# Token sums behind the attention output, a second reciprocal in PSUM, two side units moved and the last projection ahead of its fill

## The chip, the cores and the metric

One core of one Trainium2 chip runs the whole program. The metric is the device time in microseconds, the median of three runs. A profile was taken of one more execution; its own time stands beside its span in the table below.

## What is computed

Two branches read the same input `x` (2048 tokens of 512 channels) and are mixed by a gate per token. Branch A is an attention with a recurrent memory: the tokens are cut into 64 segments of 32, each segment is preceded by 8 memory rows, and the first 8 rows of a segment's output are the next segment's memory. Branch B is a layer norm and a two-layer MLP.

```python
g = sigmoid((x * gate_w).sum(-1, keepdims=True))
for s in range(64):                      # 32 heads of 128, one after the other in s
    h = concat([mem, x[32*s:32*s+32]])   # 40 rows
    q, k, v = h @ Wq, h @ Wk, h @ Wv
    p = softmax(mask(q @ k.T * scale))   # memory rows see all, token rows are causal
    o = (p @ v) @ Wo
    mem = o[:8];  outs.append(o[8:])
a = concat(outs)
b = gelu(layernorm(x) @ w1 + b1) @ w2 + b2
out = g * a + (1 - g) * b
```

## The kernel before

**Stages.** First the MLP runs in eight blocks of two token tiles (a tile is 128 tokens, T = 0 to 15) while the attention's weights load. For nine of the tiles (`DEF`) only the hidden layer is computed there and stored in DRAM (`h_dr`); their second layer is later fed into the attention loop as filler work. Then a loop runs over the 64 segments, called steps here (s = 4T + si). All instructions of an engine run in the order in which the program lists them; the order is written by hand, and the framework adds semaphores where two instructions touch the same tile. SyncE (SP) issues nearly all DMAs of the loop, in order too.

**One step.** TensorE (PE) makes q and k for 32 rows (24 tokens and the 8 memory rows; the tile's other 8 tokens per segment, the "left" ones, were made a tile ahead) into the four PSUM banks `U[0..3]`; ScalarE (ACT) casts them, VectorE (DVE) transposes them to `QT` and `KT`. Scores go in two halves of 16 heads to the banks `SbF` and `U[0]`; ACT takes the exponential into `E`; V is made in `X1` and `X2` and cast by ACT into `V`, four casts in all (L834). `E` has 56 columns per head group: columns 40 to 55 belong to the memory rows' queries. Only these are normalised before the output is made:

- `msum(i2)` sums them over the keys by a matmul with ones (`BO`), half 0 into `U[1]`, half 1 into `U[3]`; `mnorm(i2)` on DVE takes the reciprocal (L824) into `RP[i2]` and multiplies `E`'s memory columns by it (L825). `RP[0]` is a piece of the PSUM bank `SbF`, `RP[1]` the SBUF tile `RS`.
- `av` makes p @ v for all 40 rows (L291, L296), half 0 of the heads, then half 1, into the four `U` banks. It uses the normalised memory columns and the token columns as they are.
- `xsums(E, h)` sums the token columns of half h (L715) into a piece of `SbF` called `xs`. `recip_x` then takes their reciprocals into `R` (L727), writes these to DRAM (`r_dr`, L730), loads them back spread over all partitions (`Rb`, L733), and in between loads as many tiles `hm` of the deferred MLP as were used up since (L661). It copies `RP` to `R` (L735), writes the mask into `SbF` again (L260), and adds `R` into `racc` on GpSimd (POOL).
- ACT casts the memory columns of `U` to `UT` (L865) and the raw token columns to `XR` (L721). One step later POOL multiplies `XR` by `Rb` into `UT`'s token columns and into `UL` for the left tokens (`x_norm`, L745).
- `wo_pass` projects `UT` with `Wo` (L160): the memory columns of this step and the token columns of the step before. ACT casts the result to `w` in three pieces, and `new_mem` (L761, then L763 on DVE) turns each into the next step's memory rows `hT`.

**Filler.** Where a chain through ACT and DVE would leave PE idle, the step calls `run(n)`, which advances a generator `fill` made by `side(T, si)`: q, k and v of the left tokens, or the projection of `UL` (`wo_left`), four matmuls of 512 columns a unit. In step 2, where there is no earlier tile, `mlp_units(8)` stands for it: a unit is twice `next(mlp)`, a half of four matmuls of 256 columns into the bank `W` (L689). Beside that a step has two or three single halves. `hm_load4` at step 2's beginning brings four more tiles in one DMA. `WS` places two units behind V, two behind the output and two (one at si = 0) behind the projection; one follows each of the first two `new_mem`.

**The end.** Step 63 stops behind its V. Outside the loop the sums of all 32 rows are made in `SbF`, `UL` gets zeros in its unused columns (L896, POOL), `out_sel` writes the tile before, `wo_left(T, X2)` becomes the filler, DVE takes the reciprocals of all columns (L901) and normalises `E`, and `wo_pass(UT[s % 2])` projects step 62's tokens.

Of the kernel before, what the change touches and what calls it, by code (L numbers as in the profile page):

```python
# [9 lines left out]
FP32 = mybir.dt.float32  # L10
# [18 lines left out]
def kernel(ctx, tc, A_x, A_mem0, A_Wq, A_Wk, A_Wv, A_Wo, A_seg_len, B_x, B_w1, B_b1, B_w2, B_b2, gate_w, out):  # L29
    nc = tc.nc  # L30
    P = 128
    _, S, Dm = A_x.shape
# [8 lines left out]
    SPT = P // seg  # L41
# [32 lines left out]
    ep = early.enter_context(tc.tile_pool(name="ep", bufs=1))  # L74
# [31 lines left out]
    def left_x(T):  # L106
        GL = ew.tile([P, KC, LEFT, SPT], BF16, tag="GL", name="GL")
        nc.gpsimd.tensor_copy(out=GL[:].rearrange("p k c i -> p k i c"), in_=xTs[T][:].rearrange("p k (i t) -> p k i t", i=SPT)[:, :, :, RIDE:seg])
        GLs[T] = GL
# [3 lines left out]
    X1 = lps.tile([P, 512], FP32)  # L113
    X2 = lps.tile([P, 512], FP32)
    SbF = lps.tile([P, 512], FP32)
# [40 lines left out]
    def wo_group(bk, U_, n):  # L156
        j, ih = HORD[n]
        for c in range(4):
            i = 4 * ih + c
            nc.tensor.matmul(bk[32 * c:32 * c + 32, :], lhsT=U_[:, j, i, :], rhs=Wo_sb[:, 4 * i + j, :],  # L160
                             start=(n == 0), stop=(n == NW - 1), tile_position=(0, 32 * c))
# [13 lines left out]
    def left_qk(T, t, hf, bk):  # L175
        for kc in range(KC):
            qk_unit(bk, gl(T), t, hf, kc)
            if kc < KC - 1:
                yield
        def ca():  # L180
            Tb = qk_cast(bk[:])
            dve_q.append(lambda: qk_tr(Tb, QL[T % 2], hf) if t == 0 else kl_tr(Tb, T, hf))
        act_q.append(ca)
        yield
# [6 lines left out]
    def left_v(T, vb, bk):  # L191
        if vb == 0:
            VLs[T] = ew.tile([P, 4, 2, Dh], BF16, tag="VL", bufs=1, name="VL")
        for kc in range(KC):
            v_unit(bk, gl(T), vb, kc)
            if kc < KC - 1:
                yield

        def ca():
            VL = VLs[T]  # L200
            nc.scalar.copy(out=VL[:, :, vb, :], in_=bk[:].rearrange("p (a e) -> p a e", a=4))

            if vb == 1:
                vp_load(T, 0)
        act_q.append(ca)
        yield
# [8 lines left out]
    def wo_left(T, bk):  # L215
        for n in range(NW):
            wo_group(bk, UL[T % 2], n)
            if n < NW - 1:
                yield

        def ca():
            wl = cw.tile([P, Dm], BF16, tag="wl", name="wl")
            nc.scalar.copy(out=wl[:], in_=bk[:])
            wls[T] = wl
        act_q.append(ca)
        yield
# [24 lines left out]
                              in_=QL[T % 2][:].bitcast(FP32).rearrange("p a (l s) b -> p a l s b", s=SPT)[:, :, :, si])  # L251


    RS = ep.tile([P, 32], FP32)
    RP = [SbF[:, 336:368], RS[:]]


    def mask_put(i2):
        c = 4 * EW + (2 * XQ + 2 * M if i2 == 0 else 0)
        nc.vector.tensor_copy(out=(SbF, U[0])[i2][:, 0:c], in_=MkF[:, 0:c])  # L260
# [23 lines left out]
    def av(s, V, E):  # L284
        T, si = divmod(s, SPT)
        Uv = [U[j][:, 0:NG * 40].rearrange("p (i q) -> p i q", q=40) for j in range(4)]
        for i2 in range(2):
            for i in range(4 * i2, 4 * i2 + 4):
                for j in range(4):
                    q = slice(32 * j, 32 * j + 32)  # L290
                    nc.tensor.matmul(Uv[j][:, i, :], lhsT=V[q, i, :], rhs=E[q, i, 8:48],  # L291
                                     start=(i == 0), stop=False, skip_group_check=True, tile_position=(32 * j, 0))
            for j in range(4):
                q = slice(32 * j, 32 * j + 32)
                lo = slice(4 * i2, 4 * i2 + 4)
                nc.tensor.matmul(Uv[j][:, lo, :].rearrange("p i (a b) -> p i a b", b=8)[:, :, 0:5:4, :], lhsT=VP[T % 2][q, si, i2, :],  # L296
                                 rhs=E[q, lo, :].rearrange("p i (a b) -> p i a b", b=8)[:, :, 0:7:6, :],
                                 start=False, stop=True, skip_group_check=True, tile_position=(32 * j, 0))
# [329 lines left out]
    def run(n):  # L628
        for _ in range(n):
            next(fill, None)  # L630

    def chain(*gens):
        for x in gens:
            yield from x

    def side(T, si):
        gens = []
        if si == 2:
            gens = [wo_left(T - 1, X1) if T >= 1 else mlp_units(8)]
        elif T + 1 == NT:  # L640
            gens = [mlp_units(4)] if si < 2 else []
        else:
            gens = [[left_qk(T + 1, 0, 0, X1), left_qk(T + 1, 1, 0, U[3])], [left_qk(T + 1, 0, 1, X1), left_qk(T + 1, 1, 1, U[3])], [],
                    [left_v(T + 1, 0, X1), left_v(T + 1, 1, U[3])]][si]
        return chain(*gens)
# [25 lines left out]
    def mlp_out(T):  # L671
        ct = cw.tile([P, Dm], BF16, tag="o", bufs=1, name="ct")
        nc.vector.tensor_scalar(out=ct[:], in0=W[:], scalar1=omg[:, T:T + 1], scalar2=None, op0=ALU.mult)
        nc.sync.dma_start(c_dr[T * P:(T + 1) * P, :], ct[:])
# [3 lines left out]
    def mlp_outs():  # L678
        while outs:
            mlp_out(outs.pop())  # L680

    def mlp_halves():
        while hms:
            T, fc, hm, n = hms.pop(0)
            mlp_outs()
            for h in range(2):
                cc = slice(256 * h, 256 * h + 256)
                for c in range(4):
                    nc.tensor.matmul(W[32 * c:32 * c + 32, cc], lhsT=hm[:, 32 * c:32 * c + 32], rhs=w2_sb[:, fc, cc],  # L689
                                     start=(fc == 0 and h == 0), stop=(fc == FC - 1), skip_group_check=True, tile_position=(0, 32 * c))  # L690
                if h == 1:
                    owed[0] += n
                    if fc == FC - 1:
                        outs.append(T)
                yield

    def mlp_units(n):
        for _ in range(n):
            next(mlp, None)
            next(mlp, None)  # L700
            yield
# [3 lines left out]
    mlp = mlp_halves()  # L705
# [6 lines left out]
    def xsums(E, h):  # L712

        for c in range(4):
            nc.tensor.matmul(xs[32 * c:32 * c + 32, h, 0:40], lhsT=BO[:, 0:P:4], rhs=E[:, 4 * h + c, 0:40],  # L715
                             start=False, stop=True, skip_group_check=True, tile_position=(0, 32 * c))
# [7 lines left out]
    def recip_x(s):  # L724
# [9 lines left out]
        for i2 in (1, 0):  # L734
            nc.vector.tensor_copy(out=R[:, 32 * i2:32 * i2 + 32], in_=RP[i2])  # L735
        mask_put(0)
# [10 lines left out]
    def wo_pass(U_, cuts=(0, Dm), bk=W):  # L747
        for n in range(NW):
            wo_group(bk, U_, n)
        w = cw.tile([P, Dm], BF16, tag="w", bufs=8, name="w")  # L750
        for a, b in zip(cuts, cuts[1:]):
            nc.scalar.copy(out=w[:, a:b], in_=bk[:, a:b])  # L752
        return w
# [14 lines left out]
    for s in range(nseg):  # L768
        T, si = divmod(s, SPT)
        last = s == nseg - 1  # L770
        hc, hn = hT[s % 3], hT[(s + 1) % 3]
        W1, W2, W3 = WS[si]
        fill = side(T, si)
        if s + 1 < nseg:
            prep_h(s + 1)
# [25 lines left out]
        V = cx.tile([P, NG, Dh], BF16, tag="V", name="V")  # L801
        E = cx.tile([P, NG, EW], BF16, tag="E", name="E")
# [16 lines left out]
        def mnorm(i2):  # L819
            r, e = RP[i2], E[:, 4 * i2:4 * i2 + 4, 40:56].rearrange("p i (a q) -> p i a q", q=8)  # L820
            if i2 == 0:
                m = U[1][:, 320:384].rearrange("p (i a q) -> p i q a", i=4, a=2)
                nc.vector.tensor_reduce(out=r.rearrange("p (i q) -> p i q", q=8), in_=m, axis=AX.X, op=ALU.add)
            nc.vector.reciprocal(out=r, in_=U[3][:, 320:352] if i2 else r)  # L824
            nc.vector.tensor_tensor(out=e, in0=e, in1=r.rearrange("p (i q) -> p i q", q=8).unsqueeze(2).to_broadcast([P, 4, 2, 8]), op=ALU.mult)  # L825
# [32 lines left out]
        run(W1)  # L858
        if s:
            next(mlp, None)  # L860
        xsums(E, 1)
        recip_x(s)
        av(s, V, E)
        for j in (0, 2, 1, 3):
            nc.scalar.copy(out=UT[s % 2][:, j, :, 0:M], in_=U[j][:, 0:NG * 40].rearrange("p (i q) -> p i q", q=40)[:, :, 32:40])  # L865
        x_raw(s)
# [15 lines left out]
        mlp_outs()  # L882
        for _ in fill:
            pass
        if si == 3 and T + 2 < NT:
            left_x(T + 2)
        flush(dve_q, 9)
# [9 lines left out]
    for _ in out_sel(T - 1, X1):  # L897
        pass
    fill = wo_left(T, X2)
    run(3)  # L900
    nc.vector.reciprocal(out=R[:, nx], in_=SbF[:, 0:32 * NG])  # L901
    nc.scalar.activation(out=rmin[:, nx], in_=R[:, nx], func=ACTF.Copy, accum_out=tot[:, 3:4])
    ws[s - 1] = wo_pass(UT[s % 2])
    Rr = R[:, nx].rearrange("p (i q) -> p i q", q=32)
    nc.vector.tensor_tensor(out=E[:, :, 8:40], in0=E[:, :, 8:40], in1=Rr, op=ALU.mult)
    nc.vector.tensor_tensor(out=E[:, :, 0:8], in0=E[:, :, 0:8], in1=Rr[:, :, 0:8], op=ALU.mult)
# [176 lines left out]
```

## Time and profile before

| what | value |
|---|---|
| timed runs, us | 747.28, 747.86, 749.27; median 747.86 |
| profiled execution, us | 750.09 |
| its span, first to last instruction, us | 748.2 |
| granted TensorE clock, mean | 0.997 |
| busy share of the span | PE 98%, ACT 72%, DVE 60%, POOL 33% |
| hardware DMA queue of SP | 60,802 packets, 72.51 MB |

PE's share is the one that counts: an engine that is busy for 98% leaves some 15 us of idle time in all. The busy time of a matmul contains its way through the array, so short holds between small matmuls do not show as idle; they are read from the start times in the timeline.

### The profile page before, as it was taken

The page shows a single profiled execution, that of the slowest core. Times are in us where ns is not written, and L with a number is a line of the kernel's source. Part 1 is how long each engine was busy: PE and PEld are TensorE (multiplying, and loading weights), DVE is VectorE, ACT ScalarE, POOL GpSimd, SP SyncE. Part 2 cuts the span into 40 slices and gives each one's busy share as a digit, 9 for nine tenths or more (in the row PEclk, how much of TensorE's full clock was granted, in tenths as well). Part 3 has the DMA queues.
Part 4 walks back from the last instruction along what each step waited for, and adds up shares of the span by engine and source line. Part 5 has one row for each costly group of instructions (what it writes and reads, how often), then busy time and mean ns, then how long its engine had stood idle before and what let it go on. Part 6 is the DMA issues. An engine that isn't in the chain of part 4 may idle for free. (4 is left out here: it accounts for less than half of the span.)

```text
span 748.2 us, 44010 instructions
## 1 busy us (share of the span) xinstructions
PE 732.8 (98%) x19147; PEld 428.8 (57%) x19147; DVE 448.9 (60%) x1541; ACT 536.7 (72%) x1629; POOL 246.6 (33%) x515
## 2 busy tenths in 40 slices
PE   8999998999999999999999999999999999999997
PEld 5776554556565555555555555555555555555553
DVE  6877554656565555656565665556665656555554
ACT  6777765777777777777777777777777777777664
POOL 4001332332334333343234334243333343333331
PEclk9999999999999999999999999999999999999999
DMA  8999222222222323122321323231322313222221
GB/s 308 343 360 360 84 83 55 69 87 80 78 68 62 97 74 93 47 83 80 93 79 38 96 75 97 69 81 57 92 78 82 85 44 94 69 90 70 85 63 61
DMA packets 61944, 76.82 MB, mean 103 GB/s; under 512 B 26729, under 2 KB 51922, under 8 KB 60210
## 3 DMA queue, kind: packets, MB, share of 16 engines
q1 hardware_dynamic: 60802, 72.51, 31.1%
q8 instruction: 151, 2.47, 1.3%
q0 software_dynamic: 400, 0.92, 0.3%
q10 hardware_dynamic: 544, 0.52, 0.2%
q14 instruction: 47, 0.39, 0.2%
HBM read 60.21 MB, written 7.70 MB: 91 GB/s over the span
## 5 line engine op out<-in xcount | busy, mean ns | idle before, releaser
L134 ACT CAST Tb<-U 128x512 bf16<-128x512 f32 x288 | 168.8, 586 | 82.5 <-PE U L129 76.8
L745 POOL TENSOR_TENSOR UT<-XR,Rb 128x384 bf16<-128x384 bf16 x126 | 114.1, 927 | 324.6 <-DMA Rb<-r_dr 228.0
L129 PEld LDWEIGHTS <-hT 128*32 128x32 bf16 x4096 | 108.8, 97 | 97.8 <-issue 2.0
L129 PE MATMUL U<-Wq_sb,hT 128*32 128x512 bf16 x2048 | 145.9, 382 | 0.4 <-DVE hT L763 0.4
L129 PE MATMUL U<-Wk_sb,hT 128*32 128x512 bf16 x2048 | 145.2, 381 | 0.0
L148 PE MATMUL X<-Wv_sb,hT 128*32 128x512 bf16 x2048 | 142.9, 378 | 0.0
L160 PE MATMUL X<-Wo_sb,UT 128*32 128x512 bf16 x2016 | 120.8, 380 | 0.0
L834 ACT CAST V<-X 128x256 bf16<-128x256 f32 x256 | 88.7, 372 | 16.0 <-PE X L148 1.1
L138 DVE STREAM_TRANSPOSE QT<-Tb 128x256 f32<-128x256 f32 x128 | 57.0, 445 | 71.1 <-ACT Tb L134 70.9
L763 DVE CAST hT<-U 128x8 bf16<-128x8 f32 x126 | 20.8, 167 | 130.9 <-PE U L761 96.6
L160 PEld LDWEIGHTS <-UT 128*32 128x32 bf16 x2048 | 56.4, 96 | 55.7 <-issue 16.6
L721 ACT CAST XR<-U 128x256 bf16<-128x256 f32 x252 | 78.6, 438 | 0.0
L752 ACT CAST w<-X 128x128 bf16<-128x128 f32 x189 | 44.8, 310 | 41.7 <-PE X L160 41.0
L138 DVE STREAM_TRANSPOSE KT<-Tb 128x256 f32<-128x256 f32 x128 | 57.0, 445 | 25.9 <-ACT Tb L134 25.9
L737 POOL TENSOR_TENSOR racc<-racc,R 128x128 f32<-128x128 f32 x63 | 28.8, 457 | 105.7 <-DVE R L735 101.1
L148 PEld LDWEIGHTS <-hT 128*32 128x32 bf16 x2048 | 45.2, 95 | 20.6
L689 PE MATMUL W<-w_sb,hm 128*32 128x256 bf16 x728 | 50.5, 273 | 3.6 <-DMA hm<-h_dr 3.6
L865 ACT CAST UT<-U 128x64 bf16<-128x64 f32 x252 | 35.4, 227 | 25.9 <-PE U L296 25.9
L745 POOL TENSOR_TENSOR UL<-XR,Rb 128x128 bf16<-128x128 bf16 x126 | 51.5, 430 | 0.0
L809 ACT ACTIVATE E<-U 128x64 bf16<-128x64 f32 (+1 forms) x128 | 35.0, 273 | 9.3 <-PE U L271 0.4
L484 PEld LDWEIGHTS <-w_sb 128*128 128x128 bf16 (+1 forms) x352 | 34.1, 100 | 10.4
L160 PE MATMUL X<-Wo_sb,UL 128*32 128x512 bf16 x512 | 38.7, 379 | 1.0 <-POOL UL L896 1.0
(184 smaller groups left out, 1250.5 us busy)
## 6 DMA issues: line engine op xcount, KB each, us to landing
Rb<-r_dr SPq DMA_DIRECT2D x63, 512.0 KB, 3.9
Wv_sb<-in_A_Wv_dram SPq DMA_DIRECT2D x4, 1024.0 KB, 7.5
Wq_sb<-in_A_Wq_dram SPq DMA_DIRECT2D x4, 1024.0 KB, 8.5
Wk_sb<-in_A_Wk_dram SPq DMA_DIRECT2D x4, 1024.0 KB, 8.4
Wo_sb<-in_A_Wo_dram SPq DMA_DIRECT2D x4, 1024.0 KB, 12.6
VP<-VL SPq DMA_DIRECT2D x64, 64.0 KB, 3.7
hm<-h_dr SPq DMA_DIRECT2D x91, 32.0 KB, 2.6
c<-c_dr SPq DMA_DIRECT2D x16, 128.0 KB, 4.6
```

The lines of the kernel that those rows point to most:

```text
L129: nc.tensor.matmul(bk[32 * j:32 * j + 32, :], lhsT=G[:, kc, :], rhs=W5[t][:, kc, h0:h1, j, :], start=(kc == 0), stop=(kc == KC - 1), tile_ ...
L134: nc.scalar.copy(out=Tb[:], in_=bk.rearrange("p (a b e) -> p a e b", a=8, b=2))
L138: nc.vector.transpose(out=dst[:, 8 * hf:8 * hf + 8, c0:c0 + 32, :].rearrange("p a r b -> p a (r b)").bitcast(FP32), in_=Tb[:].rearrange("p ...
L148: nc.tensor.matmul(bk[32 * j:32 * j + 32, :], lhsT=G[:, kc, :], rhs=Wv5[:, kc, 4 * vb:4 * vb + 4, j, :], start=(kc == 0), stop=(kc == KC - ...
L160: nc.tensor.matmul(bk[32 * c:32 * c + 32, :], lhsT=U_[:, j, i, :], rhs=Wo_sb[:, 4 * i + j, :], start=(n == 0), stop=(n == NW - 1), tile_po ...
L689: nc.tensor.matmul(W[32 * c:32 * c + 32, cc], lhsT=hm[:, 32 * c:32 * c + 32], rhs=w2_sb[:, fc, cc], start=(fc == 0 and h == 0), stop=(fc = ...
L721: nc.scalar.copy(out=XR[:, j], in_=U[j][:, 0:NG * 40].rearrange("p (i q) -> p i q", q=40)[:, :, 0:32])
L745: nc.gpsimd.tensor_tensor(out=out[:, :, 4 * h:4 * h + 4, o:o + b - a], in0=XR[:, :, 4 * h:4 * h + 4, a:b], in1=Rb[:, h, :, :, r:r + b - a] ...
L752: nc.scalar.copy(out=w[:, a:b], in_=bk[:, a:b])
L809: nc.scalar.activation(out=E[:, 4 * i2:4 * i2 + 4, c], in_=Sb[i2][:, :, c], func=ACTF.Exp, scale=scale)
L834: nc.scalar.copy(out=V[:, i0:i0 + 2, :].rearrange("p i e -> p (i e)"), in_=(X1, X2)[vb][:, 256 * h:256 * h + 256])
L865: nc.scalar.copy(out=UT[s % 2][:, j, :, 0:M], in_=U[j][:, 0:NG * 40].rearrange("p (i q) -> p i q", q=40)[:, :, 32:40])
```

## The change

Four edits:

1. Second half's token sums: `xsums(E, 1)` and `recip_x(s)` come behind `av(s, V, E)` instead of ahead of it, in every step but the last.
2. `RS` is dropped; both memory reciprocals are pieces of `SbF` (columns 336 to 367 and 368 to 399).
3. Step 2's filler has six units instead of eight. Of the four halves that leave it, one comes at the end of step 3 and three at the end of step 4, behind the filler's rest, each followed by `mlp_outs()`, which scales and stores a finished tile of the MLP.
4. At the end `run(3)`, twelve matmuls of the `UL` projection, comes behind `wo_pass` instead of ahead of DVE's reciprocal.

```diff
-    RS = ep.tile([P, 32], FP32)
-    RP = [SbF[:, 336:368], RS[:]]
+    RP = [SbF[:, 336 + 32 * i:368 + 32 * i] for i in range(2)]
...
-            gens = [wo_left(T - 1, X1) if T >= 1 else mlp_units(8)]
+            gens = [wo_left(T - 1, X1) if T >= 1 else mlp_units(6)]
...
+        av(s, V, E)
         xsums(E, 1)
         recip_x(s)
-        av(s, V, E)
         for j in (0, 2, 1, 3):
             nc.scalar.copy(out=UT[s % 2][:, j, :, 0:M], in_=U[j][:, 0:NG * 40].rearrange("p (i q) -> p i q", q=40)[:, :, 32:40])
...
         for _ in fill:
             pass
+        for _ in range({SPT - 1: 1, SPT: 3}.get(s, 0)):
+            next(mlp, None)
+            mlp_outs()
         if si == 3 and T + 2 < NT:
...
     fill = wo_left(T, X2)
-    run(3)
     nc.vector.reciprocal(out=R[:, nx], in_=SbF[:, 0:32 * NG])
     nc.scalar.activation(out=rmin[:, nx], in_=R[:, nx], func=ACTF.Copy, accum_out=tot[:, 3:4])
     ws[s - 1] = wo_pass(UT[s % 2])
+    run(3)
```

The order of the instructions, first on DVE from the first sum of the memory columns to the mask, in a step of the loop's middle, before (the names in brackets are the engines whose semaphores a row waits for; `DVE_49` is its own; `U_119` is `U[1]`, `U_121` is `U[3]`):

```order
L823 TENSOR_REDUCE SbF<-U_119 128x32 [waits DVE_49,PE_49,Activation_49]
L824 RECIPROCAL SbF<-SbF 128x32 [waits DVE_49]
L825 TENSOR_TENSOR E<-E,SbF 128x4x16 [waits DVE_49]
L824 RECIPROCAL RS<-U_121 128x32 [waits PE_49]
L825 TENSOR_TENSOR E<-E,RS 128x4x16 [waits DVE_49,Activation_49]
L726 TENSOR_REDUCE SbF<-SbF 128x2x8 [waits PE_49]
```

The same rows now (lines are one less):

```order
L822 TENSOR_REDUCE SbF<-U_119 128x32 [waits DVE_49,PE_49,Activation_49]
L823 RECIPROCAL SbF<-SbF 128x32 [waits DVE_49]
L824 TENSOR_TENSOR E<-E,SbF 128x4x16 [waits DVE_49]
L823 RECIPROCAL SbF<-U_121 128x32 [waits DVE_49,PE_49]
L824 TENSOR_TENSOR E<-E,SbF 128x4x16 [waits DVE_49,Activation_49]
L725 TENSOR_REDUCE SbF<-SbF 128x2x8 [waits DVE_49,PE_49]
```

The rows stand in the same order; the second reciprocal and the token sums' reduction each wait for DVE's own semaphore as well, the reciprocal for the product ahead of it.

On SP, the DMAs from step 2's `recip_x` to step 3's, before:

```order
L730 DMA r_dr_78<-R 16x64
L661 DMA hm<-h_dr_69 128x128 x2
L661 DMA hm<-h_dr_70 128x128
L733 DMA Rb<-r_dr_78 128x1024
L674 DMA c_dr<-ct 128x512
L730 DMA r_dr_79<-R 16x64
L661 DMA hm<-h_dr_70 128x128 x4
L733 DMA Rb<-r_dr_79 128x1024
```

And now:

```order
L729 DMA r_dr_78<-R 16x64
L660 DMA hm<-h_dr_69 128x128 x2
L660 DMA hm<-h_dr_70 128x128
L732 DMA Rb<-r_dr_78 128x1024
L729 DMA r_dr_79<-R 16x64
L660 DMA hm<-h_dr_70 128x128 x2
L732 DMA Rb<-r_dr_79 128x1024
L673 DMA c_dr<-ct 128x512
```

Step 3 loads two tiles instead of four, and the store of the first finished deferred tile (`c_dr`) moves from behind step 2's loads to behind step 3's.

## Prediction

> **What bounds the kernel now.** I read the page first, then the windows of single steps, then the PE's waits, then the timeline of one quiet step, one disturbed step, the start and the end.
>
> ```profile
> span 748.2 us, 44010 instructions
> PE 732.8 (98%) x19147; PEld 428.8 (57%) x19147; DVE 448.9 (60%) x1541; ACT 536.7 (72%) x1629; POOL 246.6 (33%) x515
> ```
>
> TensorE is busy for 98% of the span and executes in order, so the time changes only by what PE waits for, or by the speed at which it is clocked. The profiled execution took 750.09 us, 1.85 us more than its span; the median of the timed runs is 747.86 us, 2.23 us less. I make the sum against the profile and put it on the median; the rivals come back to those 2.23 us. About 0.3% (2.2 us) is what a measurement of this kernel can tell from no change.
>
> ```profile
> core 0: us, PE busy (x) PEld busy (x) DVE busy (x) ACT busy (x) POOL busy (x), PEclk, DMA share, GB/s
> 97.08:109.35 12.27, 10.61 (x325) 6.51 (x320) 6.56 (x21) 6.69 (x22) 4.24 (x8) 1.00 0.30 87
> 109.35:123.78 14.43, 12.02 (x292) 6.14 (x288) 5.49 (x20) 7.77 (x24) 5.84 (x12) 0.88 0.25 68
> 300.62:310.81 10.19, 10.19 (x292) 5.78 (x288) 6.29 (x22) 7.67 (x24) 2.95 (x8) 1.00 0.18 66
> ```
>
> These windows run from one step's first score matmul to the next's: step 2, step 3, and step 22 as a quiet one. Steps 2 and 3 are 2.1 and 4.2 us longer than a quiet step. Why, a row of the PE's waits says (total, times, longest):
>
> ```profile
> PE W L689 <- DMA hm<-h_dr: 3.6, 3, 2.4
> ```
>
> **The start: side units.** Timeline of steps 2 to 4 (start, duration, engine, what; in brackets the idle time before it):
>
> ```profile
> 104.89 0.40 PE L689 MATMUL W<-w_sb,hm 128*32 128x256 bf16 x8 [0.89 <-DMA hm<-h_dr]
> 114.32 2.75 SPq L661 DMA_DIRECT2D hm<-h_dr  x4
> 114.94 0.62 PE L148 MATMUL U<-Wv_sb,GL 128*32 128x512 bf16 x8
> 117.96 0.29 PE L689 MATMUL W<-w_sb,hm 128*32 128x256 bf16 x4 [2.41 <-DMA hm<-h_dr]
> 119.13 1.51 PE L129 MATMUL U<-Wq_sb,hT 128*32 128x512 bf16 x12
> 131.12 0.82 PE L129 MATMUL U<-Wq_sb,hT 128*32 128x512 bf16 x12
> ```
>
> A unit is two halves of four matmuls on one `hm` tile. With eight units step 2 uses up all tiles it has. Its last units wait for loads of the same step (104.89), and step 3's third half waits 2.41 us for a tile asked for at 114.32. Soon after, the same twelve matmuls take 1.51 us at 119.13 and 0.82 us a step later: the clock, whose mean in that window is 0.88. That is 14.43 x 0.12 = 1.7 us.
>
> With six units, step 2's last two units go, and with them four halves. The tiles loaded in step 2, which its own last units used, are then left for step 3's halves, so all three waits go: -3.6, and -1.7 for the clock. The four halves come back at the ends of steps 3 and 4, where nothing waits and PE is full: a half is 0.11 us (eight matmuls take 0.40 at 104.89, four 0.29 at 117.96), +0.4. In step 2 their place between the three `new_mem` pieces becomes idle, since these wait for ScalarE's three casts anyway; that step gains only its waits. SP issues two loads fewer in step 3 in front of Rb, and the c_dr store follows Rb; both have a step of slack. Sum of the start: **-4.9 us**, with -5.4 if step 2 shortens by part of the removed halves, and -2.4 if the wait is 1.6 us and the clock stays up, as below.
>
> **The quiet step: reciprocals and sums.** From step 22, in the order DVE, ACT, PE:
>
> ```profile
> 302.45 0.37 DVE L824 RECIPROCAL SbF<-SbF 128x32 f32<-128x32 f32 x1
> 302.86 0.22 DVE L825 TENSOR_TENSOR E<-E,SbF 128x64 bf16<-128x64 bf16 x1
> 302.99 0.35 DVE L824 RECIPROCAL RS<-U 128x32 f32<-128x32 f32 x1
> 303.45 0.23 DVE L825 TENSOR_TENSOR E<-E,RS 128x64 bf16<-128x64 bf16 x1
> ```
>
> ```profile
> 303.15 0.65 ACT L834 CAST V<-X 128x256 bf16<-128x256 f32 x2
> 304.14 0.56 ACT L865 CAST UT<-U 128x64 bf16<-128x64 f32 x4 [0.35 <-PE U L296]
> ```
>
> ```profile
> 303.46 0.20 PE L715 MATMUL SbF<-E,BO 128*32 128x40 bf16 x4
> 303.73 0.34 PE L291 MATMUL U<-E,V 32*128 32x40 bf16 x16
> 304.04 0.62 PE L129 MATMUL X<-Wq_sb,GL 128*32 128x512 bf16 x8
> 304.50 0.40 PE L160 MATMUL X<-Wo_sb,UT 128*32 128x512 bf16 x4
> ```
>
> The second reciprocal starts at 302.99, 0.09 us before the first product ends (302.86 + 0.22 = 303.08): two Vector instructions without a wait between them overlap. Writing into SbF, it must now wait for that product, because the product reads SbF; the rows of the order show this wait in front of it in every step. What such a wait costs, the next pair tells: the product at 303.45 waits for the reciprocal ending 303.34 by a separate semaphore instruction and starts 0.11 us behind it. Where the wait is the instruction's own (302.82 to 302.86) it costs 0.04; the new one has two waits, so I take 0.11.
>
> So: reciprocal at 303.08 + 0.11 = 303.19; 0.37 as the PSUM-to-PSUM row above, to 303.56; product at 303.67, 0.22 as the other product, to 303.89, against 303.68 now. PE's second half of the output starts 0.05 behind the product (303.73), so at 303.94. Now it is also held inside by V's cast, which ends at 303.80; later that is no limit. What the rest then takes, a step shows in which this product came late:
>
> ```profile
> 364.36 0.81 POOL L745 TENSOR_TENSOR UL<-XR,Rb 128x128 bf16<-128x128 bf16 x2
> 364.74 0.51 DVE L825 TENSOR_TENSOR E<-E,RS 128x64 bf16<-128x64 bf16 x1
> 365.31 0.28 PE L291 MATMUL U<-E,V 32*128 32x40 bf16 x16
> 365.55 0.61 PE L148 MATMUL X<-Wv_sb,GL 128*32 128x512 bf16 x8
> 365.66 0.56 ACT L865 CAST UT<-U 128x64 bf16<-128x64 f32 x4 [0.57 <-PE U L296]
> 366.02 1.91 PE L160 MATMUL X<-Wo_sb,UT 128*32 128x512 bf16 x32
> ```
>
> From 365.31 to the next matmul 0.24; so 303.94 + 0.24 = 304.18 against 304.04: **0.14 us later in each step**, and the cast and the projection, 0.36 behind the cast in both steps, move by as much. Nothing later in the step takes it back: all else follows the projection. 63 x 0.14 = +8.8 us.
>
> The sums behind the output: four matmuls, 0.03 us of PE by their issue, inside a stretch that PE spends waiting for UT (304.18 + 0.03 + 0.43 of fill = 304.64, needed at 304.65). I cost them at nothing; uncovered they are 0.03 to 0.13 a step (303.46 to 303.59, where the output begins, is the upper end), 2 to 8 us. Before the output they covered PE time in which it waits for V anyway, so their leaving gains nothing. recip_x, the Rb load and x_norm behind them come 304.18 - 303.46 - 0.14 = 0.58 us later relative to the next step. In the late step above the UT part of x_norm is done at 364.36, 1.66 us ahead of the projection; only the few latest steps can be reached: +0.2, bounds 0 and 1.
>
> The other side of the PSUM reciprocal is that late product itself. Its durations (minimum, median, maximum, ns), and its mean:
>
> ```profile
> L825 DVE TENSOR_TENSOR E<-E,SbF x63: 220/221/223, 78.6 to 725.4; 128x64 bf16<-128x64 bf16 x63
> L825 DVEq EVENT_SEMAPHORE  x63: 21/21/21, 79.1 to 725.9; - x63
> L825 DVE TENSOR_TENSOR E<-E,RS x63: 225/226/873, 79.2 to 726.0; 128x64 bf16<-128x64 bf16 x63
> L825 DVE TENSOR_TENSOR E<-E,RS 128x64 bf16<-128x64 bf16 x63 | 17.8, 283 | 6.6
> ```
>
> With RS in SBUF it is stretched where it overlaps GpSimd's x_norm (364.36 above); with SbF it never is. That stretch goes: 63 x (283 - 226) = 3.6 us of DVE, of which in each late step (some 17 of these rows) the first 0.07 was hidden under V's cast: 3.6 - 1.2 = 2.4 us of PE. Net for the steps: 8.8 - 2.4 + 0.2 = **+6.6 us**.
>
> By the Trainium skill, "VectorE: DVE Perf Modes", section "The DRAIN you can't avoid", chained Vector instructions take the same time with or without a semaphore on each, so the new wait would be free and this sum -2.2. The rows here differ (0.09 of overlap without a wait, 0.11 of gap with one), and the rows decide.
>
> **The end.**
>
> ```profile
> 734.87 1.80 POOL L745 TENSOR_TENSOR UT<-XR,Rb 128x384 bf16<-128x384 bf16 x2 [6.66 <-DMA Rb<-r_dr]
> 737.38 0.31 POOL L896 MEMSET UL<- 128x256 bf16 x1
> 737.74 0.83 PE L160 MATMUL X<-Wo_sb,UL 128*32 128x512 bf16 x12 [0.96 <-POOL UL L896]
> 738.40 1.90 PE L160 MATMUL W<-Wo_sb,UT 128*32 128x512 bf16 x32
> 740.23 0.27 PE L291 MATMUL U<-E,V 32*128 32x40 bf16 x16
> ```
>
> The projection no longer stands behind the memset, only behind UT (736.67). With UT 0.58 later it starts at 737.30, ends at 739.03, the twelve UL matmuls (0.66) end at 739.69, and the output starts at 739.8: -0.4. With UT on time it is -1.0, with UT later still 0. I take **-0.3**.
>
> Sum: -4.9 + 6.6 - 0.3 = **+1.4 us**: 751.5 for a profiled execution, 749.3 on the median.
>
> **The rivals.** *Faster: the second reciprocal does not pay for its wait.* For it: the product it waits for ends only 0.09 us after the present start, and the skill's rule above. Against it: the 0.11 us behind the EVENT_SEMAPHORE. Then -4.9 - 2.2 - 0.3 = -7.4 us: 740.5.
>
> *Slower: the timed runs never lost what the start gives back.* Place: step 3's third half. They are 2.23 us faster than the profile, so some stall in the profile is absent from them. If the tile lands in its queue's median of 2.6 us instead of 3.6, the wait is 1.6 and the clock may stay up. It decides at the length of wait that halves the clock: 0.96 at 737.74 did not, 2.41 did. Without the clock's part the gain is 1.7 less, +3.1 us: 751.0; with the shorter wait too, 751.8. The Trainium skill, "TensorE: Matmul & The Clock Gate", Part 1, says that the gate watches a free-running window of about 3.4 us and drops the clock after an idle one. Step 3's wait was shorter than that, and dropped it.
>
> ```profile
> hm<-h_dr SPq DMA_DIRECT2D x91, 32.0 KB, 2.6
> ```
>
> **How the numbers follow.** Forecast, costs and gains cancel: 0.43. Slower rival: 0.37. Faster rival: 0.17, and 0.03 for two of the smaller gains together; so 0.20 faster. Predicted 749.3. The likeliest case by itself, from the bounds of the start (0.5) and the late UT (0.8): 747.9 to 750.1. The range takes in the slower rival's two values and the sums half uncovered, 752.2, and below it goes to 745.0; the faster rival's 740.5 is left out.
>
> **What would show it.** Right: the second L823 reciprocal starts about 0.1 us behind the first product, 0.19 later than now; the product after it is 221 ns in all 63 steps; quiet steps are 10.3 instead of 10.19 us; steps 2 and 3 near 10.3; no wait for hm and no half clock after step 1. Wrong: the reciprocal overlaps the product still, or the projection does not move with it; or a new wait for hm, Rb or VP in steps 2 to 5.

## The result and the profile after

The changed kernel takes 750.0 us (median of 19 runs, 748.20 to 752.15); the kernel before takes 747.28 us (19 runs, 745.10 to 750.75). The ratio is 1.0031, 95% interval 1.0019 to 1.0043: slower by 2.3 us, 1.4 to 3.2. The prediction said 749.3 on a kernel before of 747.86, thus +1.4. The time was right; of the terms behind it, the start gave less, and the steps' cost is made up otherwise when the edits are taken apart, as the runs below show.

The page of the profiled execution after:

```profile
span 748.2 us, 44136 instructions
PE 737.0 (98%) x19147; PEld 418.9 (56%) x19147; DVE 453.8 (61%) x1541; ACT 536.9 (72%) x1629; POOL 246.4 (33%) x515
```

Its windows of step 2, step 3, step 22 and steps 5 to 62 (columns as in the prediction):

```profile
96.67:106.97 10.30, 10.18 (x308) 6.09 (x304) 5.56 (x20) 6.70 (x22) 3.62 (x7) 1.00 0.25 71
106.97:117.36 10.39, 10.35 (x296) 5.74 (x292) 6.31 (x21) 7.67 (x24) 3.89 (x8) 1.00 0.23 62
307.12:317.41 10.29, 10.25 (x292) 5.62 (x288) 5.58 (x20) 7.28 (x23) 3.52 (x7) 1.00 0.19 54
128.19:734.69 606.50, 602.21 (x16745) 333.00 (x16740) 359.02 (x1206) 438.64 (x1373) 212.76 (x418) 1.00 0.27 76
```

Steps 5 to 62 before:

```profile
134.14:733.54 599.40, 595.97 (x16744) 341.25 (x16740) 354.61 (x1206) 438.34 (x1373) 212.99 (x418) 1.00 0.26 76
```

Steps 2 and 3 are quiet now (10.30 and 10.39 instead of 12.27 and 14.43, clock 1.00), and a quiet step is 0.14 us longer (median of steps 5 to 62: 10.33 instead of 10.19). The prediction's window 300.62 to 310.81, called step 22 there, is step 21 in the count in which 97.08 begins step 2; steps 21 and 22 took 10.19 and 10.15 us before and take 10.33 and 10.29 now. The span is the same to the tenth, 748.2: by the step starts, the MLP phase gave 0.56 us back, steps 0 to 4 5.40, the end 1.15, and steps 5 to 62 took 7.10. Yet the medians differ by 2.7 us. One of the two profiled executions is therefore not typical, and the experiments show that it is the one before, which lay 2.8 us above the median of its timed runs.

The quiet step, timeline of step 22 after:

```profile
309.34 0.22 DVE L824 TENSOR_TENSOR E<-E,SbF 128x64 bf16<-128x64 bf16 x1
309.67 0.37 DVE L823 RECIPROCAL SbF<-U 128x32 f32<-128x32 f32 x1
310.06 0.28 PE L290 MATMUL U<-E,V 32*128 32x40 bf16 x16
310.13 0.22 DVE L824 TENSOR_TENSOR E<-E,SbF 128x64 bf16<-128x64 bf16 x1
310.41 0.28 PE L290 MATMUL U<-E,V 32*128 32x40 bf16 x16
310.65 0.22 PE L714 MATMUL SbF<-E,BO 128*32 128x40 bf16 x4
310.70 0.60 PE L160 MATMUL X<-Wo_sb,UL 128*32 128x512 bf16 x8
310.76 0.56 ACT L864 CAST UT<-U 128x64 bf16<-128x64 f32 x4 [0.48 <-PE U L295]
311.13 0.82 PE L160 MATMUL X<-Wo_sb,UT 128*32 128x512 bf16 x12
```

The second reciprocal starts 0.11 us behind the first product's end (309.56 to 309.67), where before it started 0.09 ahead of it. Product, cast and projection follow it. The sums (310.65) stand right behind the output and are followed by the filler. Measured from the step's last filler matmul ahead of the output, the median start of the projection in steps 5 to 62 is 1,282 ns after and 1,133 before: 0.15 us a step.

The groups of the memory columns' product, then two of PE's waits:

```profile
L824 DVE TENSOR_TENSOR E<-E,SbF x126: 220/221/223, 78.1 to 727.4; 128x64 bf16<-128x64 bf16 x126
```

```profile
PE U L527 <- POOL ident masks.py:199: 1.5, 1, 1.5
PE X L160 <- POOL UT L744: 0.4, 1, 0.4
```

No product is stretched, no wait for `hm` is left, and one projection of the loop (0.4) waits for a late UT.

### The profile page after: what moved, and what is told of

It is laid out like the page before. It is cut to its first block, busy times and chain, and to the rows that moved or that the text cites. A ratio compares the mean times of both kernels' runs of the same rounds, so it can differ in the third digit from the quotient of the medians.

```text
span 748.2 us, 44136 instructions
## 1 busy us (share of the span) xinstructions
PE 737.0 (98%) x19147; PEld 418.9 (56%) x19147; DVE 453.8 (61%) x1541; ACT 536.9 (72%) x1629; POOL 246.4 (33%) x515
## 4 chain that ended last, share of the span: by engine, by line
PE 96%; DVE 1%; DMA 1%; issue 1%; ACT 0%; POOL 0%; DVEq 0%
PE U L129 34%; PE X L160 18%; PE X L148 17%; PE U L290 4%; PE X L129 4%; PE W L688 3%; PE U L483 2%; PE U L490 2%; PE U L148 2%; PE U L266 2%; PE SbF L714 1%; PE SbF L483 1%; PE W L483 1%; PE SbF L266 1%; PE U L295 1%
## 5 line engine op out<-in xcount | busy, mean ns | idle before, releaser
L160 PEld LDWEIGHTS <-UT 128*32 128x32 bf16 x2048 | 53.2, 96 | 57.9 <-issue 12.9
L290 PEld LDWEIGHTS <-V 32*128 32x128 bf16 x2048 | 24.9, 91 | 28.6 <-DVE SbF L823 19.1
```

## The experiments

Each run is compared with runs of the kernel before on the same chip (medians 745.7 to 747.3 in the several groups); I use the ratios, and turn a difference of ratios into us by 747.

### The units alone

```diff
-            gens = [wo_left(T - 1, X1) if T >= 1 else mlp_units(8)]
+            gens = [wo_left(T - 1, X1) if T >= 1 else mlp_units(6)]
...
+        for _ in range({SPT - 1: 1, SPT: 3}.get(s, 0)):
+            next(mlp, None)
+            mlp_outs()
```

> The kernel before with the six units and the moved halves alone. Theory of the prediction: the start gives back 4.9 us in every run, so about 743 us, a ratio of 0.9934 to before. The slower rival (the timed runs lose less at step 3 than the profiled execution did): 2.1 to 3.1 us, a ratio of 0.996 to 0.997. In the trace both want steps 2 and 3 near 10.3 us, no wait for hm and no half clock after step 1, and quiet steps as before (10.15 to 10.19 us).

743.27 us, ratio 0.9953 (0.9933 to 0.9972): -3.5 us, between the two. Steps 2 and 3 of its trace:

```profile
96.22:106.53 10.31, 10.19 (x308) 6.24 (x304) 5.56 (x20) 6.69 (x22) 3.61 (x7) 1.00 0.26 76
106.53:116.86 10.33, 10.33 (x296) 5.87 (x292) 6.18 (x21) 7.67 (x24) 4.43 (x9) 1.00 0.25 80
```

Against the first profile of the kernel before, steps 0 to 4 together are 5.9 us shorter (51.87 against 57.76). The timed runs gain less, so most of them must lose less before.

### The kernel before, profiled twice more

> The kernel before, unchanged, profiled once more. The slower rival's mechanism: the wait for hm in step 3 and the half clock behind it differ from execution to execution, so steps 2 and 3 together take anything from 23 to 27 us here (26.7 in the first profile, 24.0 in the run with the PSUM reciprocals alone, where the clock stayed at 1.00). If the start's loss is fixed: 26.5 to 26.9 again.

> As the run before it: a further execution of the unchanged kernel, for the spread of steps 2 and 3. By the slower rival they add up to 23 to 27 us, and the execution's time follows them; if the start's loss is fixed, 26.5 to 26.9 whatever the time.

743.12 and 744.90 us. Steps 2 and 3, and PE's wait for `hm`, of the first:

```profile
96.70:107.90 11.20, 10.54 (x325) 6.58 (x320) 6.28 (x21) 6.69 (x22) 4.11 (x8) 1.00 0.29 84
107.90:120.01 12.11, 10.34 (x292) 5.64 (x288) 5.45 (x20) 7.76 (x24) 3.94 (x9) 1.00 0.23 70
```

```profile
PE W L689 <- DMA hm<-h_dr: 2.3, 2, 1.8
```

and of the second:

```profile
96.90:107.65 10.75, 10.47 (x325) 6.53 (x321) 6.26 (x21) 6.69 (x22) 4.19 (x8) 1.00 0.26 78
107.65:119.78 12.13, 10.34 (x292) 5.60 (x288) 5.45 (x20) 7.77 (x24) 3.81 (x9) 1.00 0.24 70
```

```profile
PE W L689 <- DMA hm<-h_dr: 1.8, 1, 1.8
```

Steps 2 and 3 add up to 23.3 and 22.9 us instead of 26.7. The wait in step 3 is 1.8 us instead of 2.4, and the clock stays at 1.00. This is the slower rival's mechanism, in the same code (the two ran on a chip where the timed runs of this kernel had a median of 745.84; the chip of the first profile is not known). The timed runs bear it out: half a clock for 3.41 us, which is what the first profile shows (119.01 to 122.43), takes 0.0023 off the mean granted clock, and of the 62 timed runs of this kernel in the four groups of the experiments 51 had a mean of 0.999 or 1.000, and only 11 one of 0.998 or less. By this mechanism the units are worth 2 to 2.5 us in these two executions (steps 0 to 4: 54.37 and 53.77 against 51.87) and 5.9 in the one that the prediction was made from. The start explains 3.4 and 4.0 of the 7.0 and 5.2 us by which these executions are shorter than that one; the rest lies in steps 5 to 62 (597.43 and 598.63 against 599.40), the end and the MLP phase.

### The PSUM reciprocals alone

```diff
-    RS = ep.tile([P, 32], FP32)
-    RP = [SbF[:, 336:368], RS[:]]
+    RP = [SbF[:, 336 + 32 * i:368 + 32 * i] for i in range(2)]
```

> The kernel before with both reciprocals written into SbF and nothing else. If a tensor engine read of SbF waits for the whole bank's last reader, the second pair of token sums, which still stands in front of the output here, waits for the second product: it ends at 0.51 us behind the step's last mlp matmul, sums 0.56, output 0.69, which holds back the output by some 0.4 us a step, 63 x 0.40 = 25 us, a ratio of 1.034. If the sums don't wait for it, only the product's own delay is left: 8.8 - 2.4 = 6.4 us, 1.009. If the second reciprocal doesn't pay for its wait (faster rival): -2.2 us, 0.997.

769.28 us, ratio 1.0290 (1.0266 to 1.0315): +21.7 us. Its timeline in step 22:

```profile
317.25 0.37 DVE L823 RECIPROCAL SbF<-U 128x32 f32<-128x32 f32 x1
317.72 0.22 DVE L824 TENSOR_TENSOR E<-E,SbF 128x64 bf16<-128x64 bf16 x1
317.99 0.22 PE L714 MATMUL SbF<-E,BO 128*32 128x40 bf16 x4 [0.28 <-DVE E L824]
```

The sums write other columns of SbF than the product reads, but the framework keeps order by the tile, and SbF is one tile: the sums wait until the product has ended (317.94), and the output stands behind them on PE. A quiet step is 10.64 us, 0.45 longer. So edits 1 and 2 are one edit: with both reciprocals in SbF the sums must go behind the output.

### The sums alone

```diff
+        av(s, V, E)
         xsums(E, 1)
         recip_x(s)
-        av(s, V, E)
```

> The kernel before with the second pair of token sums, the reciprocal of the sums and the Rb load behind the output's matmuls, and the second reciprocal still in RS. By the prediction's costing: nothing (ratio 1.000), uncovered 2 to 8 us (1.003 to 1.011). Rival: the Rb load comes some 0.5 us later, so GpSimd's x_norm lies over the product with RS in more steps than before; each product stretched costs up to 0.5 us, so with 17 instead of 35 stretched products 3 to 8 us more. The trace tells them apart by the durations of the product with RS (mean 283 ns before).

751.91 us, ratio 1.0068 (1.0043 to 1.0093): +5.1 us. Groups of the product with RS (durations minimum, median, maximum) and their mean, and PE's wait for it:

```profile
L825 DVE TENSOR_TENSOR E<-E,RS x63: 224/235/966, 78.9 to 727.5; 128x64 bf16<-128x64 bf16 x63
```

```profile
L825 DVE TENSOR_TENSOR E<-E,RS 128x64 bf16<-128x64 bf16 x63 | 20.7, 328 | 6.6
```

```profile
PE U L291 <- DVE E L825: 2.2, 6, 0.6
```

The mean went from 283 to 328 ns; 26 of the 63 products take over 300 ns, where before it was 15. In steps 5 to 62, `r_dr` is stored 0.57 us later, as the prediction had worked out, and x_norm is still at work when the product with RS starts (2.82 us into the step) in 45 of 58 steps instead of 23.

### The whole change without the second reciprocal in PSUM

```diff
-    RP = [SbF[:, 336 + 32 * i:368 + 32 * i] for i in range(2)]
+    RS = ep.tile([P, 32], FP32)
+    RP = [SbF[:, 336:368], RS[:]]
```

(against the changed kernel)

> The whole change without the second reciprocal in SbF (it stays in RS). By the prediction's terms: -4.9 - 0.3 + 0.2 = -5.0 us against before, a ratio of 0.993, and 6.4 us less than the changed kernel. By the slower rival's start: -2.2 to -3.2 us, 0.996 to 0.997. If the later x_norm stretches more products with RS: 3 to 8 us of that is lost, 0.999 to 1.004, and the second reciprocal in SbF then pays for itself.

747.34 us, ratio 1.0002 (0.9984 to 1.0019). So the second reciprocal in PSUM costs 2.2 us, not 6.4, and what units and end gain is lost already without it. Steps 5 to 62, and the mean of the product with RS:

```profile
128.07:731.77 603.70, 598.82 (x16744) 330.43 (x16740) 359.00 (x1206) 438.65 (x1373) 213.41 (x418) 1.00 0.27 76
```

```profile
L825 DVE TENSOR_TENSOR E<-E,RS 128x64 bf16<-128x64 bf16 x63 | 20.4, 324 | 6.6
```

### Units and end alone

```diff
-        av(s, V, E)
         xsums(E, 1)
         recip_x(s)
+        av(s, V, E)
```

(against the kernel of the run above)

> The kernel before with the six units, the moved halves and the projection ahead of the last output weights' fill; sums and reciprocals as before. By the terms as the first four runs show them: -3.5 us for the units (743.3 against 746.9) and -0.3 to -1.0 for the end: 742.3 to 743, a ratio of 0.994. Were the loss of the run without the PSUM reciprocal (ratio 1.000) not the sums' but an interplay of units and end, this one would stand at 1.000 too.

742.42 us (739.84 to 743.54), ratio 0.9950 (0.9933 to 0.9968). This is the lowest ratio of all versions (that of the units alone, 0.9953, lies within its interval), 3.7 us below the kernel before and 0.8% below the changed one. Steps 5 to 62, and the mean of the product with RS:

```profile
128.14:726.74 598.60, 595.93 (x16745) 340.76 (x16740) 354.48 (x1206) 438.36 (x1373) 212.57 (x418) 1.00 0.26 77
```

```profile
L825 DVE TENSOR_TENSOR E<-E,RS 128x64 bf16<-128x64 bf16 x63 | 16.5, 262 | 6.6
```

So, by the ratios, each edit against the run without it: units -0.47% (-3.5 us), end -0.03% (-0.2), sums +0.52% (+3.9), second reciprocal in PSUM +0.29% (+2.2).

### Why do the sums cost: two runs without x_norm

In these two, GpSimd's products of `XR` and `Rb` are left out; the columns that they fill stay zero.

```diff
         nc.gpsimd.memset(UT[i][:, :, :, M:32], 0.0)
+        nc.gpsimd.memset(UL[i][:], 0.0)
...
-        XR, Rb = XRs.pop(s), Rbs.pop(s)[:].rearrange("p (c j) (h q) -> p h j c q", c=4, h=2)
-        for out, o, a, b, r in ((UT[(s + 1) % 2], M, LEFT, 32, 0), (UL[T % 2], LEFT * si, 0, LEFT, 32 - LEFT)):
-            for h in range(2):
-                nc.gpsimd.tensor_tensor(out=out[:, :, 4 * h:4 * h + 4, o:o + b - a], in0=XR[:, :, 4 * h:4 * h + 4, a:b], in1=Rb[:, h, :, :, r:r + b - a], op=ALU.mult)
+        XRs.pop(s), Rbs.pop(s)
```

> The whole change without the second reciprocal in SbF, and without GpSimd's x_norm products, which are left out (their place stays zero). Theory: with no x_norm every product with RS takes 225 to 227 ns, so the sums behind the output cost only their own 0.02 to 0.03 us a step (1 to 2 us), and this is 3 to 6 us below the same kernel with x_norm (747.3), thus 741.5 to 744.5. Rival: the sums cost by standing on PE behind the output: then leaving x_norm out changes only what late UT and the last step lose, 1 us or less: 746.3 or more.

> The changed kernel without GpSimd's x_norm products (left out as in the run above). Its second product is never stretched, so leaving x_norm out takes only what late UT and the end lose, 1 to 2 us: 748 to 749. Against the same without the second reciprocal in SbF: the wait's price alone, 0.14 us x 63 = 8.8 us by the prediction's step, with nothing to set against it; if the wait costs no more than the 2.7 us by which the changed kernel stood above the one without it (750.0 against 747.3), the two differ by 2.7.

745.85 us (ratio 1.0000, 0.9989 to 1.0011) and 751.75 (1.0087, 1.0071 to 1.0102). The first lies above the 741.5 to 744.5 of the theory and just under the rival's 746.3, the second above the 748 to 749 expected; by these times alone, leaving x_norm out gained nothing. The trace says why: the edit brought a wait of its own. Products with RS in the first of the two, then the place behind the last `new_mem`, step 26:

```profile
L823 DVE TENSOR_TENSOR E<-E,RS x63: 225/226/227, 78.7 to 723.5; 128x64 bf16<-128x64 bf16 x63
```

```profile
L129 PEldq EVENT_SEMAPHORE  x63: 51/51/51, 83.1 to 727.3; - x63
```

```profile
353.30 0.20 PE L759 MATMUL SbF<-SelM,w 128*32 128x8 bf16 x8
353.47 0.40 PE L129 MATMUL U<-Wq_sb,hT 128*32 128x512 bf16 x4
```

The same place in the run of units and end alone:

```profile
L160 PEldq EVENT_SEMAPHORE  x63: 51/51/51, 80.2 to 720.4; - x63
```

```profile
352.45 0.20 PE L761 MATMUL SbF<-SelM,w 128*32 128x8 bf16 x8
352.52 0.40 PE L129 MATMUL U<-Wq_sb,hT 128*32 128x512 bf16 x4
```

Once a step a weight load of PE waits for GpSimd and for another engine too, and has a semaphore instruction of its own in front of it. It stood in front of the projection, where PE waits for UT anyway; without x_norm it moved to the first q matmul, and there 0.17 us pass instead of 0.07 from the start of the one row to that of the next. In three of four steps the rest of the step became 0.07 us longer by the medians, some 47 x 0.07 = 3.3 us. The other part of the step became shorter: from the last filler matmul ahead of the output to the projection, 1,171 ns in the mean of steps 5 to 61 instead of 1,228 with x_norm, 3.3 us in all, which is what the stretch had taken. The semaphore instruction costs both runs the same, so their difference stands: 5.9 us by the medians, 6.5 by the ratios, which is the new wait with nothing to set against it. With x_norm it was 2.2. Less 3.3, the runs come to some 742.5 and 748.4, inside what the theory expected, but that is worked out, not measured.

### The places exchanged

```diff
-    RP = [SbF[:, 336 + 32 * i:368 + 32 * i] for i in range(2)]
+    RS = ep.tile([P, 32], FP32)
+    RP = [RS[:], SbF[:, 336:368]]
```

(against the changed kernel)

> The whole change, but with the two places exchanged: the first reciprocal in RS (SBUF), the second in SbF. The second then needs no wait for the first product (which reads RS), and the second product reads no SBUF reciprocal. Theory: a read of two SBUF operands beside GpSimd's x_norm is what stretches a product, so the second product is 221 ns in all 63 steps, the second reciprocal again starts before the first product ends, and quiet steps are near 10.17 to 10.2 us: 5 to 7 us less than the changed kernel, 743 to 745 us, 0.995 to 0.998 of before. Rival: the first product is now stretched as often, holds the second reciprocal behind it, and all or half of that comes back: 746 to 748 us.

753.79 us, ratio 1.0104 (1.0083 to 1.0125). The theory's 743 to 745 fell, and the rival's 746 to 748 was too low. Mean of the product with RS, now the first, and step 22:

```profile
L825 DVE TENSOR_TENSOR E<-E,RS 128x64 bf16<-128x64 bf16 x63 | 31.7, 503 | 6.6
```

```profile
309.76 0.82 POOL L745 TENSOR_TENSOR UL<-XR,Rb 128x128 bf16<-128x128 bf16 x2
310.26 0.40 DVE L825 TENSOR_TENSOR E<-E,RS 128x64 bf16<-128x64 bf16 x1
310.58 0.35 DVE L824 RECIPROCAL SbF<-U 128x32 f32<-128x32 f32 x1
311.04 0.22 DVE L825 TENSOR_TENSOR E<-E,SbF 128x64 bf16<-128x64 bf16 x1
```

The first product stands 0.6 us earlier in the step, where x_norm is at work in nearly every step: 50 of 63 take over 300 ns, and all behind them on DVE moves along. What the theory said of the mechanism held (the second product takes 220 to 223 ns throughout, and the second reciprocal overlaps the first product's end by 0.08, 310.66 to 310.58); I had not asked where in the step x_norm lies.

### Rb later, the sums in their old place

First with SP's `hm` loads ahead of the `r_dr` store, on units and end alone:

```diff
-        nc.sync.dma_start(r_dr[s % 2][:], R[0:P:8, 8 * NG:RW])
         hm_load(owed[0])
         owed[0] = 0
+        nc.sync.dma_start(r_dr[s % 2][:], R[0:P:8, 8 * NG:RW])
```

> The run with units and end alone (742.4 us, 0.995), with one edit: SP issues the hm loads owed ahead of the r_dr store instead of behind it, so that the Rb load and x_norm come some 0.6 us later, as they do in the changed kernel, while the token sums stay ahead of the output on PE. Theory: the loss of the sums' move is for the larger part that lateness (products with RS stretched by x_norm, first scores held up), so this run shows products with RS longer in the mean than the 262 ns of units and end alone, some 30 of 63 stretched instead of 17, and 1.5 to 4 us more: 744 to 746.5. Rival: it is the four matmuls' own place on PE; then 742.4 within 0.6.

742.24 us, ratio 0.9954 (0.9937 to 0.9971). It decides nothing: the store still started 6.22 us ahead of the next step's first scores at the median (6.21 without the edit), because SP had been waiting for the reciprocal and issued the `hm` load in that time. Then with the reciprocal issued twice:

```diff
         nc.vector.reciprocal(out=R[:, 8 * NG:RW].rearrange("p (h q) -> p h q", h=2), in_=xs[:, :, 16:48])
+        nc.vector.reciprocal(out=R[:, 8 * NG:RW].rearrange("p (h q) -> p h q", h=2), in_=xs[:, :, 16:48])
```

> Units and end alone (742.4 us, 0.995) with the reciprocal of the token sums issued twice in a row on VectorE, so that the r_dr store, the Rb load and x_norm come some 0.5 us later, as in the changed kernel, and the token sums keep their place ahead of the output on PE. (The run before it did not do that: its r_dr store still started 6.2 us ahead of the next step.) Theory: the lateness of x_norm is the larger part of what moving the sums costs (3.9 us timed): products with RS stretched in some 30 of 63 steps instead of 17, their mean 310 to 330 ns, and 744 to 746. Rival: it is the sums' place behind the output on PE: 742.4 within 0.6.

747.32 us, ratio 1.0025 (1.0009 to 1.0041), 5.6 us above units and end alone and above the 744 to 746 expected. The store starts 5.66 us ahead of the next step, as after (5.64). Steps 5 to 62, the product with RS, and PE's wait for it:

```profile
128.28:730.96 602.68, 597.67 (x16744) 341.26 (x16740) 390.35 (x1264) 438.55 (x1373) 213.00 (x418) 1.00 0.27 76
```

```profile
L826 DVE TENSOR_TENSOR E<-E,RS 128x64 bf16<-128x64 bf16 x63 | 21.3, 338 | 6.9 <-ACT V L835 0.5
```

```profile
PE U L291 <- DVE E L826: 2.8, 10, 0.4
```

With the sums ahead of the output, x_norm's lateness alone makes 25 products longer than 300 ns (11 in units and end alone) and costs most of what the sums' move costs: in the profiles it takes 4.1 us in steps 5 to 62, where the sums' move took 5.1 (602.68 and 603.70 against 598.60). The end of this profile is 1.5 us longer as well (15.24 against 13.75 us from step 63's first scores), but not by x_norm, which ends no later there; SP waits 1.7 us for a last semaphore, as it does 1.6 us in the run with the places exchanged. So not all of the 5.6 us is lateness. The added reciprocal itself, 0.6 us of DVE a step, is not what costs: the undisturbed step 22 takes 10.15 us in both. The projection's median start, 1,137 ns behind the last filler matmul here and 1,131 in units and end alone, did not move: the loss lies in the disturbed steps. The sums' own place shows in that median: 1,157 in the whole change without the second reciprocal in PSUM, 0.024 us a step, 1.5 us in all.

## Why the prediction was right, and where not

**The quiet step, second reciprocal.** Right in mechanism, and close in each number: gap 0.10 (forecast 0.11), reciprocal 0.37, product 0.22 in all 126, projection 0.15 later (0.14). Without the sums' 0.024 it is 0.124 x 63 = 7.8 us against +8.8. The Trainium skill's rule that I weighed there ("VectorE: DVE Perf Modes", section "The DRAIN you can't avoid": a semaphore costs chained Vector instructions nothing) does not hold in this trace: 0.09 us of overlap became 0.10 of gap. The faster rival fell with it.

**The sums behind the output.** This step failed. "I cost them at nothing", with 2 to 8 us if uncovered, looked at the four matmuls on PE; those cost 1.5 us. The larger cost was in the next sentence: x_norm 0.58 later, "+0.2, bounds 0 and 1". I asked only whether the late UT holds up the projection, and not what else x_norm meets on its way. It meets the product with RS, though the row of 873 ns that I had quoted was just that. While the second reciprocal stays in RS, the sums cost 3.9 us by the ratios, and the run with the reciprocal twice shows that lateness alone costs some 4 us in the loop.

**The stretch that goes.** I took 2.4 us from the stretch as it was before the sums moved. Against the kernel before, that holds: in its three executions the steps whose product took over 300 ns reached the projection 1.9, 2.7 and 2.6 us later in all than at the median. With x_norm later it is larger (mean 324 instead of 283 ns, 3.5 us by the same count), and the second reciprocal in SbF removes all of it. By the steps that leaves 7.8 - 3.5 = 4.3 us net instead of 6.4; the timed runs say 2.2, and the difference is not explained. The two deviations cancel in the whole change, since a product that reads SbF was not stretched however late x_norm came: so there the forecast's mechanism, the wait less the old stretch, is the one at work, and with the sums' own place it makes 7.8 - 2.4 + 1.5 = 6.9 us. The scores and filler ahead of the output are held up in some steps as well, 2.3 us in all after and 0.3 to 1.3 in the three executions before; without x_norm it is 1.6 and 2.2, so its lateness is not shown to be the cause. Against before, the whole came to 7.1 us in 58 steps, 7.7 in 63 by the profiles, and to 6.1 by the ratios; forecast 6.6.

**The start.** The edit did what I said (steps 2 and 3 at 10.30 and 10.39, no wait, no half clock), but -4.9 us is its worth against one execution. In the timed runs it is -3.5, interval -5.0 to -2.1. The slower rival's mechanism is the one that the further profiles and the granted clocks show: its gain of 3.2, with the clock staying up, is nearest. Its 751.0 lies 1 us above the measured 750.0: by the ratios the start gave 0.3 more than its number and the steps cost 0.5 less (3.9 + 2.2 against 6.6).

**The end.** Forecast -0.3, bounds -1.0 and 0; measured -1.15 between the two profiles, and -0.2 by the ratios of the two runs with and without it. The end of the kernel before itself lasts 13.56 to 14.70 us in three executions, by when the last x_norm comes.

By the ratios the four terms are -3.5, -0.2, +3.9 and +2.2 us; they add up to the whole by the way they were taken, and each of the last three is uncertain by some 1.6 to 1.9 us. That the forecast of 749.3 lies only 0.7 us from 750.0 is in part luck: the start gave 1.4 less than forecast, the steps cost 0.5 less, and the median of the kernel before came out 0.6 lower than the one it was put on.

## What to carry to other kernels

A wait that an edit makes later must be followed to every engine that its successor shares something with, not only to the next reader: here the later Rb load cost next to nothing where it was needed (one projection waited 0.4 us) and, as long as the second reciprocal lay in RS, some us where GpSimd's work then lay over a Vector instruction on the critical chain. A term read from the trace of before (a stretch, a stall) is measured under the old schedule; when another edit of the same change moves its cause, price the two together. And before a stall of one profiled execution is booked as a gain, look whether the timed runs are faster than that execution; two more profiles of the old kernel settle it.

## What the runs showed of the hardware

- A Vector product with two inputs in SBUF that is stretched beside a product of GpSimd ends about 0.08 us behind it: 310.26 + 0.40 = 310.66 above, against 309.76 + 0.82 = 310.58. Of the 220 products of E with RS that took over 300 ns in all traces, 189 end 0.07 to 0.09 us behind the GpSimd product that was running when they started, and the other 31 as far behind one that started within 0.05 us of them. With one input in PSUM the product took 220 to 223 ns in every step of every run. By the Trainium skill, "SBUF — State Buffer", section "Who interferes with whom", the two engines share a port pair, and the one that issues second is blocked in full, not slowed down; the trace agrees. That makes the place in the step decisive: the same product is longer than 300 ns in 10 to 28 of 63 steps at 2.8 us into the step, and in 50 of 63 at 2.2.
- Whether the clock halves hung on a fraction of a microsecond of PE's wait for `hm`. With the eight units five executions were profiled: in two the longest wait was 2.4 us, and step 3's clock was 0.88; in three it was 1.7 or 1.8, and the clock 1.00. The second execution of the first kind is that of the sums alone, step 3 and the wait:

```profile
108.29:122.75 14.46, 12.04 (x292) 5.94 (x288) 5.47 (x20) 7.77 (x24) 5.39 (x11) 0.88 0.22 68
```

```profile
PE W L689 <- DMA hm<-h_dr: 3.3, 3, 2.4
```

By the Trainium skill, "TensorE: Matmul & The Clock Gate", Part 1, the clock drops after an idle window of about 3.4 us that runs free of the program. Here a wait of 2.4 us was enough. The traces show such windows themselves, and how much of one must be idle: in all 14, the changes of the granted clock lie whole multiples of 3.413 us apart. When each trace is cut into such windows from its first change on, the 16 in which PE was idle for 1.89 us or more (14 of them at the end of the program) were each followed by half the clock, and none of the other 3,023 was, in which it was idle for 1.78 us at most. Around step 3's wait the idle time in one window was 2.36 and 2.07 us in the two executions that lost the clock, and at most 1.78, 1.42 and 1.36 in the three that kept it. So where a wait falls counts beside its length.
- A semaphore instruction of its own in front of a weight load cost PE 0.10 us where nothing covered it (0.17 against 0.07 from start to start of the same two groups) and next to nothing in front of the projection, whose median start is 1,154 ns behind the last filler matmul without it and 1,157 with it (the whole change without the second reciprocal in PSUM, without and with x_norm).
